# Hi casts of the second FFN's weight sums on GpSimd, three output pairs in the first pass, and a line of their own for gate tiles

## The chip, the cores and the metric

The kernel runs on one core of one Trainium2 chip. The metric is the device time of one execution in microseconds (us), lower is better. Several runs are timed; their median is the time of the kernel. A profiled execution gives the trace.

The engines have short names in the trace: PE is TensorE's matmul and PEld its weight load, DVE is VectorE, ACT is ScalarE, POOL is GpSimd, SP is SyncE, which issues the DMAs. Each engine works through its instructions in the order in which the program has them; an instruction that must wait holds all that stand behind it on its engine.

## The reference

Windowed attention (4 batches, 8 heads, 576 positions, head dimension 64, a window of 64), then two feed-forward networks over the 2304 tokens of 512 features, all in float32:

```python
attn = softmax(where(0 <= i - j < 64, q @ k.T / 8, -1e9)) @ v   # per batch and head
x = attn, heads side by side                                    # 2304 x 512
h = x @ w_in                                                    # 512 -> 2048
x = where(h > 0, h, exp(min(h, 0)) - 1) @ w_out                 # ELU, 2048 -> 512
xn = x / sqrt(mean(x * x, -1) + 1e-6) * rms_g
g, val = xn @ w_gate, xn @ w_val                                # 512 -> 1536 each
out = (g * sigmoid(g) * val) @ w_out2                           # 1536 -> 512
```

## The kernel before

**Precision.** Every operand of the large products is split in two: Hi is the value cast to a narrower matmul type (F32R), Lo is the rest, value minus Hi, cast likewise. A product is then three matmul groups, Hi Hi, Hi Lo and Lo Hi. A split is therefore a cast and a subtraction that reads the cast's result.

**First pass.** Five blocks of tokens (384, 384, 512, 512, 512). In each, 16 steps f make the input product (PE L729), the ELU on ScalarE and VectorE (L767, L769, L771), its split (Hi cast L775, Lo L777), and two steps later the output product (PE L806), which adds up in four PSUM banks y. Attention for the tokens of later blocks is scattered between these steps. When a block ends, its four banks are copied (L839), and the RMS norm follows within the next block; the normed tokens go to DRAM. The 32 split weight units of this FFN stay in SBUF in the 32 slots of the pool "wu". In the last block they come free one by one, and the same slots then serve the second FFN.

**Second pass.** The second FFN works on three superblocks of 768 tokens and computes each 2 x 2 block product with seven products of sums and differences instead of eight (a Strassen scheme; ORDER lists the seven). So it needs seven sums of every weight tile, each split in Hi and Lo. These sums are prepared once, during the first pass and the start of the second, and spilled to DRAM: 12 gate and value units (prep_steps) into pspill, and 6 output pairs (prep_out) into ospill. The second pass loads them back (p_load, o_load). For each superblock it runs three pairs of gate and value tiles (pair, PE L1141), then a half of the output products over these three pairs (outs, PE L1237), then the same for the other three. The third to fifth output pair (counted from 0) serve only the second half. Gate results are kept in tiles G, in slots of "wu"; outs makes sums of them (L1184) and splits these (L1199 Hi, L1202 Lo, the latter on VectorE or GpSimd as the order chooses).

**Preparing a unit or a pair.** Two raw tiles are loaded (L663), their low half words are moved by GpSimd (L669), a join on VectorE (L676) makes the float32 tile in one of two buffers "wm", GpSimd makes four sums of quarter tiles (L1016), and put_out does for each of the seven sums: a Hi cast on ScalarE (L972), a Lo subtraction on GpSimd (L974), and a store by SP (L977), out of one of two buffers "stg". Raw tiles lie in one of three buffers "big4", which the norm uses as well, or, for the output pairs prepared in the second pass, in slots of "wu". A load step calls Feeder.load, which loads every raw tile up to its own that hasn't been loaded.

**The order.** The program order of all engines is made by a list scheduler, class Plan, before anything is built. Each step has a cost for each engine that may run it, the tiles it reads and writes, and for a load the time to landing. Plan.run takes the step that can start first; among those within 0.1 us it prefers the one with the longest tail of work behind it, to which plan.sooner(by, ...) adds some us. Buffers of a pool are counted; Plan.queue puts some tiles in a line, in which a tile gets a buffer only when all those named before it have had theirs. The costs are only used to make the order: on the chip the engines run that order with semaphores.

Of the kernel before, what the change touches and what calls it, by code (L numbers as in the profile page):

```python
# [29 lines left out]
class Plan:  # L30
# [15 lines left out]
        fn()  # L46
        self.early = 0.0

    def add(self, costs, fn, reads=(), writes=(), load=0.0, rows=128, name=None):
        x = Step()  # L50
        x.early = self.early
        x.costs = {e: c * self.MARGIN.get(e, 1.0) for e, c in costs.items()}
        x.fn, x.index, x.load, x.rows, x.name = fn, len(self.steps), load, rows, name
        x.deps, x.tiles = {}, []
        for r in reads:
            key, off = r if isinstance(r[0], tuple) else (r, 0.0)
            self.tile_of(x, key)
            if key in self.writer:
                self.dep(x, self.writer[key], off)
            self.readers.setdefault(key, []).append(x.index)  # L60
        for w in writes:
            key, off = w if isinstance(w[0], tuple) else (w, 0.0)
            self.tile_of(x, key)
            for y in [*self.readers.pop(key, ()), *([self.writer[key]] if key in self.writer else ())]:
                if y != x.index:
                    self.dep(x, y, off)
            self.writer[key] = x.index
        self.steps.append(x)
# [10 lines left out]
    def queue(self, t):  # L79

        if t[0] == "wu":
            return ("raw" if t[1][0] == "r" else "wl" if t[1][0] in ("p", "o") else
                    "wu" if isinstance(t[1], tuple) else None)
        if t[0] == "y" and isinstance(t[1][0], int):
            return "y"
        return None if t[0] in "wy" else t[0]
# [66 lines left out]
    def put(self, x, e, t):  # L153
# [14 lines left out]
        self.free[e] = t + c  # L168
        if x.load:
            self.dma = max(t + 1.6, self.dma) + x.load  # L170
            self.end[x.index] = self.dma + 0.3
        else:
            self.end[x.index] = t + c
        for tile in x.tiles:
# [61 lines left out]
def kernel(  # L236
# [17 lines left out]
    nc = tc.nc  # L254
# [89 lines left out]
    plan = Plan()  # L344
# [620 lines left out]
    def put_out(dst, dkey, src, key, sg, cost={"POOL": 0.82}):  # L965


        def tile_():
            return get((*sg, 0), lambda: mp.tile(
                [128, 2, 256], F32R, tag=sg[0], name=sg[0], bufs=2))  # L970

        add({"ACT": 0.41}, lambda e: nc.scalar.copy(out=tile_()[:, 0, :], in_=src()),  # L972
            reads=[key], writes=[(*sg, "h")])
        add(cost, lambda e: on(e).tensor_tensor(  # L974
            out=tile_()[:, 1, :], in0=src(), in1=tile_()[:, 0, :].bitcast(F32),
            op=ALU.subtract), reads=[key, (*sg, "h")], writes=[(*sg, "l")])
        add({"SP": 0.55}, lambda e: nc.sync.dma_start(out=dst, in_=tile_().bitcast(F32)),  # L977
            reads=[(*sg, "h"), (*sg, "l")], load=0.7, writes=[dkey])

    def prep_steps(t):  # L980

# [51 lines left out]

    def prep_out(i):
        ns = [2 * preps.index(("o", i)) + a for a in range(2)]
        raw = [("wu", ("ro", n), 0) if i >= 4 else ("big4", ("r", n), 0) for n in ns]
        m = [(f"wm{n % 2}", ("p", n)) for n in ns]
        one, sk = ("wm2", "top", 0), ("sw", ("o", i), 0)

# [214 lines left out]
    for f in range(F1):  # L1254
        if f + 1 < F1:
# [3 lines left out]
    OF = [f for i in range(NP2) for f in (i, i + NP2)]  # L1259
    nblk = len(BLOCKS1)  # L1260
    preps = [("p", t) for t in range(4 * (nblk - 2))] + [("o", i) for i in range(NP2)]
    PREP = [{}, *[{f: 4 * b + n for n, f in enumerate((3, 6, 9, 12))}
              for b in range(nblk - 2)],
            {5: 12, 8: 13, 11: 14, 13: 15}]
    w2src = []
    for kind, i in preps:
        for a in range(2):
# [76 lines left out]
    for sb in range(NSB):  # L1344
# [3 lines left out]
        def put(at, fn):  # L1348
            todo.setdefault(at, []).append(fn)
# [15 lines left out]
        if sb == 0:  # L1365
            norm = norm_steps(nblk - 1, BLOCKS1[-1], tok0 - BLOCKS1[-1], True)
            next(norm)
            put(2, lambda: plan.sooner(100.0, lambda: next(norm, None)))
            for i in range(4, NP2):
                put(2 * (i - 4), lambda i=i: plan.sooner(0.0, lambda: prep_out(i)))  # L1370
        if sb + 1 < NSB:
            put(38, lambda: x_load(sb + 1))
            for j, fn in enumerate(x_items(sb + 1)):
# [102 lines left out]
```

## Time and profile before

| | |
|---|---|
| median of 3 runs | 917.25 us (915.98 to 918.17) |
| profiled execution | 915.95 us, span from the first to the last instruction 914.2 us |
| mean granted TensorE clock | 0.994 of full speed |
| TensorE busy with matmuls | 891.2 us, 97% of the span |
| VectorE, ScalarE, GpSimd busy | 632.4, 489.3 and 345.9 us |
| first pass, second pass | the first output product of the last block ends near 502 us; the second FFN's products run from there on |

A busy time is the time in which an engine has an instruction running; TensorE's matmuls are pipelined, so its busy time does not say that each runs at its best. A granted clock of 1.00 is 2.4 GHz, 0.5 is 1.2 GHz; a stretch between has some of both. In a timeline, the bracket behind a row gives how long the engine was idle before it and whose work ended that idle time.

### The profile page before, as it was taken

How to read it: one execution, taken by the hardware profiler on the slowest of the kernel's cores; microseconds unless marked ns; L12 is line 12 of the kernel's file. 1: busy time of each engine (PE TensorE's matmuls, PEld its weight loads, DVE VectorE, ACT ScalarE, POOL GpSimd, SP SyncE). 2: the span in 40 equal slices, each digit the busy share in tenths (PEclk: the TensorE clock that was granted, in tenths of full speed). 3: DMA queues.
4: the chain of work that ended last, by engine and by line, in shares of the span. 5: the costliest groups of instructions: out<-in, count | busy, mean ns of one | idle time of the engine just before them, and what ended most of it. 6: DMA issues, size and time to landing. Idle time of an engine off the chain costs nothing.

```text
span 914.2 us, 16974 instructions
## 1 busy us (share of the span) xinstructions
PE 891.2 (97%) x6063; PEld 824.5 (90%) x6063; DVE 632.4 (69%) x1294; ACT 489.3 (54%) x1191; POOL 345.9 (38%) x379
## 2 busy tenths in 40 slices
PE   8899999999999999999998998999999999999998
PEld 7888999998888888888886998899999999999998
DVE  6899977555656567557755588879758379667476
ACT  6788676765557565546434645445333344333432
POOL 3777632334433442443146557623112113112121
PEclk9999999999999999999998999999999999999999
DMA  9995227735376344837664985994997675988742
GB/s 232 324 330 141 58 81 226 197 108 149 128 240 170 115 141 128 245 129 228 228 235 159 325 303 208 334 410 172 378 359 270 227 244 166 392 300 290 242 149 70
DMA packets 156164, 201.87 MB, mean 221 GB/s; under 512 B 82608, under 2 KB 108720, under 8 KB 156080
## 3 DMA queue, kind: packets, MB, share of 16 engines
q1 hardware_dynamic: 156080, 200.79, 67.2%
q8 instruction: 48, 0.79, 0.4%
q14 instruction: 36, 0.29, 0.1%
HBM read 158.29 MB, written 42.47 MB: 220 GB/s over the span
## 4 chain that ended last, share of the span: by engine, by line
PE 85%; DVE 7%; DMA 3%; ACT 3%; issue 1%; POOL 1%; SPq 0%; DVEq 0%; POOLq 0%; ACTq 0%
PE w L729 19%; PE y L806 19%; PE y L1141 16%; PE w L1141 12%; PE y L1237 8%; PE w L1237 4%; PE w L555 2%; PE w L476 2%; PE w L540 1%; PE w L421 1%; DVE wm L676 1%; DMA ospill<-stg 1%; DVE g L1202 1%; DVE g L777 1%; DMA kq<-in_k_dram 1%
## 5 line engine op out<-in xcount | busy, mean ns | idle before, releaser
L806 PE MATMUL y<-g,wu 128*128 128x512 f32 (+1 forms) x960 | 216.9, 376 | 7.0 <-ACT g L775 4.4
L729 PE MATMUL w<-x,wu 128*128 128x512 f32 (+1 forms) x960 | 212.4, 372 | 2.1 <-POOL wu L692 1.0
L806 PEld LDWEIGHTS y<-g,wu 128*128 128x128 f32 x960 | 174.5, 190 | 32.4 <-ACT g L775 5.3
L729 PEld LDWEIGHTS w<-x,wu 128*128 128x128 f32 x960 | 173.6, 188 | 26.9 <-issue 1.7
L1141 PE MATMUL y<-xw,pu 128*128 128x384 f32 x648 | 121.1, 335 | 0.0
L1141 PEld LDWEIGHTS y<-xw,pu 128*128 128x128 f32 x648 | 112.9, 188 | 0.0
L1114 DVE TENSOR_TENSOR c<-c,w 128x384 f32<-128x384 f32 x72 | 39.7, 553 | 86.0 <-PE w L1141 81.7
L974 POOL TENSOR_TENSOR stg<-wm,stg 128x256 fp32r<-128x256 f32 x70 | 58.7, 840 | 97.1 <-ACT stg L972 95.9
L771 DVE SCALAR_TENSOR_TENSOR e<-e,w 128x512 f32<-128x512 f32 (+1 forms) x80 | 50.2, 631 | 51.9 <-ACT e L769 51.3
L1202 POOL TENSOR_TENSOR g<-slot,g 128x384 fp32r<-128x384 f32 x21 | 27.0, 1286 | 151.9 <-ACT g L1199 108.2
L777 DVE TENSOR_TENSOR g<-e,g 128x512 fp32r<-128x512 f32 (+1 forms) x80 | 67.6, 849 | 24.3 <-ACT g L775 23.7
L1141 PE MATMUL w<-xw,pu 128*128 128x384 f32 x432 | 81.5, 336 | 0.0
L1141 PEld LDWEIGHTS w<-xw,pu 128*128 128x128 f32 x432 | 75.9, 189 | 0.2
L767 ACT ACTIVATE e<-w 128x512 f32<-128x512 f32 (+1 forms) x80 | 44.2, 552 | 57.8 <-PE w L729 57.0
L974 POOL TENSOR_TENSOR stg<-sw,stg 128x256 fp32r<-128x256 f32 x50 | 40.8, 817 | 77.9 <-ACT stg L972 77.9
L1118 DVE TENSOR_TENSOR slot<-slot,c 128x384 f32<-128x384 f32 x108 | 64.0, 604 | 0.9
L1109 ACT COPY c<-y 128x384 f32<-128x384 f32 x72 | 34.4, 480 | 52.1 <-PE y L1141 49.1
L1237 PE MATMUL y<-wu,g 128*128 128x256 f32 x432 | 57.8, 287 | 3.6 <-DVE g L1202 3.4
L1237 PEld LDWEIGHTS y<-wu,g 128*128 128x128 f32 x432 | 54.8, 194 | 4.8 <-DVE g L1202 4.2
L775 ACT CAST g<-e 128x512 fp32r<-128x512 f32 (+1 forms) x76 | 43.7, 575 | 24.4 <-DVE e L771 24.0
L1129 ACT ACTIVATE slot<-c 128x384 f32<-128x384 f32 x54 | 28.4, 526 | 52.0 <-DVE c L1114 50.6
L692 POOL TENSOR_TENSOR wu<-wm,wu 128x512 fp32r<-128x512 f32 x32 | 49.8, 1579 | 14.5 <-ACT wu L687 11.5
(169 smaller groups left out, 1552.5 us busy)
## 6 DMA issues: line engine op xcount, KB each, us to landing
pu<-pspill SPq DMA_DIRECT2D x126, 512.0 KB, 5.9
wu<-ospill SPq DMA_DIRECT2D x60, 512.0 KB, 6.7
pspill<-stg SPq DMA_DIRECT2D x84, 256.0 KB, 2.1
tmp<-in_moe_w_out_dram SPq DMA_DIRECT2D x23, 511.8 KB, 6.8
ospill<-stg SPq DMA_DIRECT2D x36, 256.0 KB, 3.2
tmp<-in_moe_w_in_dram SPq DMA_DIRECT2D x16, 511.0 KB, 7.4
vw<-in_v_dram SPq DMA_DIRECT2D x27, 256.0 KB, 4.2
big<-in_moe_w_gate_dram SPq DMA_DIRECT2D x12, 511.0 KB, 3.8
```

The lines of the kernel that those rows point to most:

```text
L692: nc.gpsimd.tensor_tensor(out=u[:, 1, :], in0=m, in1=u[:, 0, :].bitcast(F32), op=ALU.subtract)
L729: nc.tensor.matmul(pt[:, :n], lhsT=wt[:, a, kk * 128:(kk + 1) * 128], rhs=xs[kk][:, c, :n], start=(i == 0), stop=(i == len(seq) - 1))
L767: add({"ACT": of_n(0.49, n)}, lambda e: nc.scalar.activation(out=et(), in_=ph(), func=AF.Relu, scale=-1.0), reads=ws, writes=[e_])
L771: add({"DVE": of_n(0.56, n)}, lambda e: nc.vector.scalar_tensor_tensor(out=et(), in0=et(), scalar=-1.0, in1=ph(), op0=ALU.add, op1=ALU.max ...
L775: lambda e: copy_on(e)(out=gt()[:, 0, :n], in_=et()),
L777: add({"DVE": of_n(0.68 if b else 0.93, n)}, lambda e: nc.vector.tensor_tensor(out=gt()[:, 1, :n], in0=et(), in1=gt()[:, 0, :n].bitcast(F3 ...
L806: nc.tensor.matmul(py[m][:, :n], lhsT=wt[:, a, m * 128:(m + 1) * 128], rhs=g[:, c, :n], start=(first and i == 0), stop=(last and i == 2))
L974: add(cost, lambda e: on(e).tensor_tensor(out=tile_()[:, 1, :], in0=src(), in1=tile_()[:, 0, :].bitcast(F32), op=ALU.subtract), reads=[key ...
L1114: add({"DVE": 0.55}, lambda e: nc.vector.tensor_tensor(out=c_of(ck), in0=c_of(ck), in1=at(bk), op=ALU.add), reads=[bk], writes=[ck])
L1118: add({"DVE": 0.55}, lambda e: nc.vector.tensor_tensor(out=et(), in0=et(), in1=src_of(sk), op=ALU.mult), reads=[sk], writes=[ek])
L1141: nc.tensor.matmul(at(bk), lhsT=p_of(sb, i, j)[:, qi, a, kk * 128:(kk + 1) * 128], rhs=X_of(sb, j, kk)[:, x, :], start=(first and n == 0), ...
L1237: nc.tensor.matmul(at(bk)[:, (m % 2) * 256:(m % 2) * 256 + 256], lhsT=S_of(jp, i)[:, a, m * 128:(m + 1) * 128], rhs=w[:, x * 256:(x + 1) * ...
```

## The change

The Hi cast of each weight sum is issued on GpSimd (gpsimd.tensor_copy) instead of ScalarE; the scheduler counts 0.82 us for it instead of 0.41. The scheduler counts 0.5 us more until the store of a sum has landed. The last block has three output pairs in its list, not four; the fourth is prepared in the second pass with its raw tiles in slots of "wu", as the last two were, and these three are put at places 0, 12 and 24 of the first superblock, each with 40 us of preference, where the last two had places 0 and 2 and none. Tiles G have a line of their own in Plan.queue; before, they stood in the line of all other slots. PREP for the middle blocks is the same list written out.

```diff
--- before.py
+++ after.py
@@ -46,11 +46,12 @@
         fn()
         self.early = 0.0
 
-    def add(self, costs, fn, reads=(), writes=(), load=0.0, rows=128, name=None):
+    def add(self, costs, fn, reads=(), writes=(), load=0.0, rows=128, name=None, slow=0.0):
         x = Step()
         x.early = self.early
         x.costs = {e: c * self.MARGIN.get(e, 1.0) for e, c in costs.items()}
         x.fn, x.index, x.load, x.rows, x.name = fn, len(self.steps), load, rows, name
+        x.slow = slow
         x.deps, x.tiles = {}, []
         for r in reads:
             key, off = r if isinstance(r[0], tuple) else (r, 0.0)
@@ -80,7 +81,7 @@
 
         if t[0] == "wu":
             return ("raw" if t[1][0] == "r" else "wl" if t[1][0] in ("p", "o") else
-                    "wu" if isinstance(t[1], tuple) else None)
+                    "G" if t[1][0] == "G" else "wu" if isinstance(t[1], tuple) else None)
         if t[0] == "y" and isinstance(t[1][0], int):
             return "y"
         return None if t[0] in "wy" else t[0]
@@ -168,7 +169,7 @@
         self.free[e] = t + c
         if x.load:
             self.dma = max(t + 1.6, self.dma) + x.load
-            self.end[x.index] = self.dma + 0.3
+            self.end[x.index] = self.dma + 0.3 + x.slow
         else:
             self.end[x.index] = t + c
         for tile in x.tiles:
@@ -969,13 +970,13 @@
             return get((*sg, 0), lambda: mp.tile(
                 [128, 2, 256], F32R, tag=sg[0], name=sg[0], bufs=2))
 
-        add({"ACT": 0.41}, lambda e: nc.scalar.copy(out=tile_()[:, 0, :], in_=src()),
+        add({"POOL": 0.82}, lambda e: nc.gpsimd.tensor_copy(out=tile_()[:, 0, :], in_=src()),
             reads=[key], writes=[(*sg, "h")])
         add(cost, lambda e: on(e).tensor_tensor(
             out=tile_()[:, 1, :], in0=src(), in1=tile_()[:, 0, :].bitcast(F32),
             op=ALU.subtract), reads=[key, (*sg, "h")], writes=[(*sg, "l")])
         add({"SP": 0.55}, lambda e: nc.sync.dma_start(out=dst, in_=tile_().bitcast(F32)),
-            reads=[(*sg, "h"), (*sg, "l")], load=0.7, writes=[dkey])
+            reads=[(*sg, "h"), (*sg, "l")], load=0.7, slow=0.5, writes=[dkey])
 
     def prep_steps(t):
 
@@ -1033,7 +1034,7 @@
 
     def prep_out(i):
         ns = [2 * preps.index(("o", i)) + a for a in range(2)]
-        raw = [("wu", ("ro", n), 0) if i >= 4 else ("big4", ("r", n), 0) for n in ns]
+        raw = [("wu", ("ro", n), 0) if i >= 3 else ("big4", ("r", n), 0) for n in ns]
         m = [(f"wm{n % 2}", ("p", n)) for n in ns]
         one, sk = ("wm2", "top", 0), ("sw", ("o", i), 0)
 
@@ -1259,9 +1260,7 @@
     OF = [f for i in range(NP2) for f in (i, i + NP2)]
     nblk = len(BLOCKS1)
     preps = [("p", t) for t in range(4 * (nblk - 2))] + [("o", i) for i in range(NP2)]
-    PREP = [{}, *[{f: 4 * b + n for n, f in enumerate((3, 6, 9, 12))}
-              for b in range(nblk - 2)],
-            {5: 12, 8: 13, 11: 14, 13: 15}]
+    PREP = [{}, {3: 0, 6: 1, 9: 2, 12: 3}, {3: 4, 6: 5, 9: 6, 12: 7}, {3: 8, 6: 9, 9: 10, 12: 11}, {5: 12, 8: 13, 11: 14}]
     w2src = []
     for kind, i in preps:
         for a in range(2):
@@ -1366,8 +1365,8 @@
             norm = norm_steps(nblk - 1, BLOCKS1[-1], tok0 - BLOCKS1[-1], True)
             next(norm)
             put(2, lambda: plan.sooner(100.0, lambda: next(norm, None)))
-            for i in range(4, NP2):
-                put(2 * (i - 4), lambda i=i: plan.sooner(0.0, lambda: prep_out(i)))
+            for i, at in zip(range(3, NP2), (0, 12, 24)):
+                put(at, lambda i=i: plan.sooner(40.0, lambda: prep_out(i)))
         if sb + 1 < NSB:
             put(38, lambda: x_load(sb + 1))
             for j, fn in enumerate(x_items(sb + 1)):
```

## Rows read from the trace of the kernel before

**Rows 1.** The page's part 1: busy us (share) and instructions by engine.

```profile
PE 891.2 (97%) x6063; PEld 824.5 (90%) x6063; DVE 632.4 (69%) x1294; ACT 489.3 (54%) x1191; POOL 345.9 (38%) x379
```

**Rows 2.** Busy us (x instructions) by stretch and engine, granted clock, DMA share, GB/s.

```profile
200.00:300.00 100.00, 100.00 (x685) 82.49 (x685) 58.44 (x156) 61.85 (x165) 40.10 (x51) 1.00 0.56 164
450.00:500.00 50.00, 45.59 (x192) 36.98 (x191) 27.10 (x37) 21.35 (x43) 25.94 (x31) 0.95 0.62 218
500.00:545.00 45.00, 45.00 (x251) 44.21 (x250) 29.00 (x48) 25.62 (x55) 23.95 (x27) 0.98 0.85 296
545.00:580.00 35.00, 30.27 (x218) 29.26 (x218) 30.66 (x43) 14.76 (x37) 21.07 (x22) 0.95 0.73 268
```

**Rows 3.** Timeline, first FFN's end: start us, us, engine, line, work, [idle before <-releaser].

```profile
467.55 0.89 POOL L974 TENSOR_TENSOR stg<-sw,stg 128x256 fp32r<-128x256 f32 x1 [1.03 <-ACT stg L972]
...
469.58 3.05 SPq L663 DMA_DIRECT2D tmp<-in_moe_w_out_dram  x2
...
475.44 0.86 SPq L977 DMA_DIRECT2D ospill<-stg  x2
...
480.75 0.41 ACT L972 CAST stg<-wm 128x256 fp32r<-128x256 f32 x1 [8.53 <-DMA ospill<-stg]
...
482.01 0.69 DVE L676 SCALAR_TENSOR_TENSOR wm<-big,top 128x512 int32<-128x512 int32 x1 [9.07 <-POOL stg L974]
...
489.41 3.02 PE L806 MATMUL y<-g,wu 128*128 128x512 f32 x12 [0.83 <-ACT g L775]
...
496.01 5.49 PE L806 MATMUL y<-g,wu 128*128 128x512 f32 x12 [3.58 <-ACT g L775]
```

**Rows 4.** Chain that ended last, same end and later: start us, us, what.

```profile
475.44 5.23 DMA ospill<-stg
...
482.00 4.28 DMA ospill<-stg
...
620.25 2.16 PE y L1237 x18
```

**Rows 5.** Timeline, first output products of the second FFN (columns as in rows 3).

```profile
551.24 0.62 PE L1237 MATMUL y<-wu,g 128*128 128x256 f32 x3 [1.12 <-DVE g L1202]
...
552.52 2.56 PE L1237 MATMUL y<-wu,g 128*128 128x256 f32 x13 [0.66 <-DVE g L1202]
...
554.88 3.12 PE L1237 MATMUL y<-wu 128*128 128x256 f32 x18
...
561.21 2.18 PE L1237 MATMUL y<-wu 128*128 128x256 f32 x16 [0.80 <-DVE wu L1202]
...
578.35 1.34 PE L1237 MATMUL w<-wu,g 128*128 128x256 f32 x9 [2.13 <-DVE slot L1399]
```

**Rows 6.** Groups of instructions by line: busy us, mean ns | idle before them <-releasers.

```profile
L974 POOL TENSOR_TENSOR stg<-wm,stg 128x256 fp32r<-128x256 f32 x70 | 58.7, 840 | 97.1 <-ACT stg L972 95.9 <-DMA ospill<-stg 0.9
...
L972 ACT CAST stg<-wm 128x256 fp32r<-128x256 f32 x70 | 28.1, 403 | 22.7 <-DMA ospill<-stg 15.7 <-DMA pspill<-stg 4.5 <-DVE wm L676 2.2
...
L669 POOL CAST top<-big 128x512 f16<-128x512 bf16 x29 | 24.8, 855 | 60.0 <-DMA big<-in_moe_w_val_dram 29.0 <-DMA big<-in_moe_w_out_dram 18.1 <-DVE wm L676 9.0
...
L1300 POOL MEMSET top<- 128x512 f32 x1 | 0.5, 522 | 0.0
```

**Rows 7.** Waits by pairs over the span: us in total, times, longest us.

```profile
POOL stg L974 <- ACT stg L972: 173.8, 72, 12.1
...
ACT stg L972 <- DMA ospill<-stg: 19.3, 11, 8.5
```

**Rows 8.** Lines L777, L771: duration ns min/median/max, first and last start us, shapes.

```profile
L777 DVE TENSOR_TENSOR g<-e,g x80: 544/693/1650, 32.2 to 496.0; 128x512 fp32r<-128x512 f32 x48, 128x384 fp32r<-128x384 f32 x32
...
L771 DVE SCALAR_TENSOR_TENSOR e<-e,w x80: 540/680/690, 30.3 to 494.6; 128x512 f32<-128x512 f32 x48, 128x384 f32<-128x384 f32 x32
```

**Rows 9.** Lines L676, L1202 (columns as in rows 8), some of their forms.

```profile
L676 DVE SCALAR_TENSOR_TENSOR wm<-tmp,top x7: 679/683/1223, 497.6 to 581.5; 128x512 int32<-128x512 int32 x7
...
L1202 DVE TENSOR_TENSOR wu<-slot,wu x9: 543/546/1080, 552.4 to 565.5; 128x384 fp32r<-128x384 f32 x9
```

## The prediction

> **What bounds the kernel now.** I read the page's first part, then the busy times by stretch, the timelines of the two stretches that show idle TensorE, the chain of waits through them, and the waits summed by pairs.
>
> TensorE is busy for 891.2 of 914.2 us [rows 1]. The stretches tell the rest [rows 2]: from 200 to 300 us TensorE is idle for nothing at a granted clock of 1.00; from 450 to 500 it is busy for 45.6 of 50 us, and from 545 to 580 for 30.3 of 35, both at a mean granted clock of 0.95, that is, part of the time at 1.2 instead of 2.4 GHz. So what a change outside the matmuls can give back lies in these two stretches, and what it can spoil is the first pass, which loses nothing today.
>
> Loss A is the end of the first FFN [rows 3]. TensorE waits 0.83 us and 3.58 us for an activation's Hi cast, and then the product at 496.01 takes 5.49 us where the one at 489.41 took 3.02 us: 2.47 us to the lower clock, which fell behind the wait. A = 0.83 + 3.58 + 2.47 = 6.9 us. Its cause stands in the same timeline. ScalarE's cast L972 for the spilled weight sums starts at 480.75 after 8.53 us of waiting for a store, and the ELU's first step L767 stands behind it in ScalarE's queue. VectorE has its own wait to the same moment: the join L676 at 482.01 waits 9.07 us for GpSimd's subtraction L974, because the join overwrites what L974 reads, and the ELU's step L771 stands behind the join. The store itself was late: GpSimd had finished its source at 467.55 + 0.89 = 468.44, but SP issued it at 475.44, behind raw loads (L663) which waited for weight slots, and the chain of waits runs through it and the next store for 5.23 and 4.28 us [rows 4].
>
> Loss B is the first half of the second FFN's output products [rows 5]: waits of 1.12, 0.66 and 0.80 us for VectorE's Lo parts, and the lower clock, 18 matmuls in 3.12 us against 2.16 at full clock [rows 4], and 13 in 2.56 us against 13/18 of 2.16 = 1.56. B = 2.58 + 0.96 + 1.00 = 4.5 us. Loss C is the 2.13 us wait at 578.35 for VectorE's sum L1399. VectorE is busy for 30.7 of the 35 us there [rows 2].
>
> **The change, part by part.** *The casts.* 126 casts leave ScalarE (seven for each of 12 gate and value units and 6 output pairs), each about 403 ns [rows 6]: 51 us less of an engine that is 54% busy, worth nothing by itself. What counts is the wait before them, 19.3 us for output stores [rows 7], which holds the ELU; on GpSimd it holds only the preparation, since in the blocks after the first no ELU step runs there. The trace has no 128x256 cast on GpSimd. From below it is half of the 128x512 memset's 522 ns, 0.26 us; from above the two-input subtraction of the same size, 0.84 us; the nearest row is GpSimd's 128x512 cast of 855 ns, half of which is 0.43 us [rows 6]. I take 0.43: 126 x 0.43 = 54 us (33 to 106) more on an engine that is busy for 345.9 of 914.2 us [rows 1]. One pair has two 0.855 casts, four sums and seven subtractions at about 0.84 us, 10.9 us; with seven casts it has 13.9. Four pairs per first-pass block are 56 us of the 100 in [rows 2], three in the last block 42 us of some 55. So it fits. In exchange GpSimd's 173.8 us of waits for ScalarE's cast [rows 7] shrink: cast and subtraction now follow each other on one queue, with the store's wait ahead of both. What is queued behind that wait on GpSimd is the next sums and, in the second pass, Lo parts (L1202).
>
> The cost on VectorE: its activation Lo L777, which reads two SBUF tiles, takes 544 to 1650 ns, median 693, while L771, which reads one of its two tiles from PSUM, stays between 540 and 690, its two widths [rows 8]. So GpSimd's work stretches VectorE's two-tile work. By the Trainium skill (SBUF — State Buffer, Who interferes with whom) VectorE with two SBUF inputs and a GpSimd instruction that reads SBUF exclude each other for a whole instruction, and ScalarE has ports of its own; these rows agree, and by that rule moving the cast off ScalarE is a loss for VectorE wherever it is full. By another page of the Trainium skill (GPSIMD Engine Reference, Engine selection) one-input work there runs near line rate; no row shows a cast of this size, and an estimate from it, 256 elements at 1.2 GHz, would be 0.21 us and the sum over 126 casts 27 us instead of 54. In the first pass VectorE is 58% busy and the output product comes two steps behind the ELU, so I cost the stretching at nothing there; were that cover gone, a collision would cost up to 0.4 us on TensorE (the cast's length). In the full stretch from 545 to 580 about seven casts of one pair fall, 7 x 0.43 = 3.0 us, of which I let a third reach TensorE: +1.0 us (between 0 and 3.0).
>
> *Three pairs instead of four in the last block.* Less moves than the words say. All 12 output raws are loaded in order, and a load step that comes up early loads all before it as well, into its own kind of buffer: seven of the twelve are joined out of weight slots ("tmp"), where four were meant to be, and these joins run from 497.6 to 581.5 us [rows 9]. So before the change only two pairs and the start of a third are prepared in the first pass. Now six raws are meant for slots and counted there. The load, join, cast, sum and store instructions stay as many, SP's too. Zero, with a gain contained in A: fewer loads that the order did not count stand in SP's queue ahead of the stores.
>
> *The store's extra 0.5 us and the new cast cost in the order of work.* Both enter the order written out, not the chip. A staged sum is counted 0.41 + 0.5 = 0.9 us later, seven of them 6.4 us, about one ELU step of the last block (two products, 2 x 3.02 us [rows 3]). The join that waited 9.07 us is therefore put behind one ELU step more, and about 2.7 us of its wait would be left, less than the two steps by which the output product trails. With the cast gone from ScalarE's queue and the join later in VectorE's, both holds of A go: -6.9 us (between -6.9 and 0).
>
> *Own order of places for activations.* Gate tiles no longer stand in one line with raw loads. In the pairs' stretch from 500 to 545 us TensorE is busy for 45.0 of 45 us [rows 2], so I take 0. The sixth pair's raws still stand in line behind second-output tiles, whose Lo parts first run at 552.4 [rows 9]. Loaded from there (some 5 us, like the stores of rows 4), joined and prepared for 13.9 us with as much again of store waits, it is out by 590; its consumer starts at 620.25 [rows 4]. That slack of 30 us covers it; beyond it each us would be one of TensorE.
>
> **The sum.** A -6.9, B +1.0, C 0, the first pass 0: -5.9 us. The profiled execution took 915.95 us (span 914.2 and 1.75 around it), so 910.05; it lies 1.3 us below the median 917.25 of the runs, and against that median I predict 911.3 us.
>
> **The rivals.** *R1, the hold only changes queue.* The store is late because of SP, so GpSimd waits for it instead of ScalarE, the join still waits for GpSimd to 482, and the ELU's L771 is as late as before. For it: VectorE's wait of 9.07 us ends at the same moment as ScalarE's 8.53 [rows 3], so freeing one alone gives nothing. Against: the order of the joins changes too. Time: 917.25 + 1.0 - about 1 = 917.3.
>
> *R2, the second pass becomes the bound (slower).* With cast and subtraction both on GpSimd, the order gives its Lo parts to VectorE, and the two pairs prepared around 545 to 580 us collide with it. VectorE has 35 - 30.7 = 4.3 us to spare there. Four Lo parts moved, at 0.55 us unhindered [rows 9], are 2.2 us; 14 casts x 0.43 = 6.0 us of collisions, 8.2 in all, 3.9 over the room, and a further clock fall like the one in B, 1.0 to 2.0 us: +5.4. With A unrecovered as in R1, 922.6; it decides from the point where VectorE's busy share there passes 35 us. For it: B and C are waits for VectorE already. Against: the casts may be short and ScalarE, with 14.8 of 35 us, can take copies.
>
> *R3, everything late goes.* A, B and C together, 6.9 + 4.5 + 2.1 = 13.5: 903.8. For it: the last-block norm gets its buffers earlier when a pair less holds them. Against: B's VectorE is full for other reasons.
>
> **How the numbers follow.** The forecast has 0.48 (907 to 915), R1 0.18, R2 0.21, R3 0.13. About 0.2% (1.8 us) is what a measurement can tell from no change. Forecast and R3 count as faster, 0.61; R1 as the same, 0.18; R2 as slower, 0.21. The range takes R3's 903.8 with 2 us for an unknown first half, and R2's 922.6: 902 to 923.
>
> **What would show it.** Right: no L972 on ScalarE; a cast on GpSimd of about 0.43 us; no wait of several us before L767 between 450 and 500 us, joins there waiting under 3 us, and a granted clock of 1.00. Wrong: TensorE's waits for L775 at the block's end as long as before (R1), more than 2.6 us of waits for L1202 in the second pass's first output half (R2), any idle TensorE between 200 and 450 us, or a cast near 0.84 us, which would make a first-pass block's GpSimd 67 us and bring the joins near the block's end.

## The result and the profile after

| | before | after |
|---|---|---|
| median | 916.62 us (914.88 to 918.17, 4 runs) | 904.98 us (903.76 to 906.14, 4 runs) |
| profiled execution, its span | 915.95 and 914.2 us | 906.14 and 904.4 us |
| TensorE without work in the span | 914.2 - 891.2 = 23.0 us | 904.4 - 887.7 = 16.7 us |

The changed kernel is faster, by a ratio of 0.9876 [0.9855, 0.9898]. That is 11.6 us where 5.9 us were forecast: inside the range, in the forecast direction, but twice its size, and next to R3's 903.8. The profiled execution after is the longest of its four, so its trace shows 9.8 us of the 11.6.

Part 1 of the page of the kernel after (busy us, share, instructions by engine) answers to [rows 1]:

```profile
PE 887.7 (98%) x6063; PEld 821.6 (91%) x6063; DVE 638.2 (71%) x1302; ACT 450.0 (50%) x1068; POOL 398.3 (44%) x494
```

ScalarE has lost 39 us and GpSimd has gained 52: that part of the change did what it says. TensorE's own busy time fell by 3.5 us for as many matmuls, with a mean granted clock of 0.996 instead of 0.994. The same four stretches as in [rows 2] (busy us and instructions of PE, PEld, DVE, ACT, POOL, then granted clock, DMA share, GB/s) say where it came from:

```profile
200.00:300.00 100.00, 100.00 (x684) 82.27 (x683) 60.36 (x154) 53.43 (x138) 58.30 (x86) 1.00 0.60 171
450.00:500.00 50.00, 50.00 (x229) 42.29 (x228) 24.54 (x35) 20.49 (x37) 35.34 (x52) 1.00 0.62 211
500.00:545.00 45.00, 43.54 (x255) 42.34 (x253) 40.98 (x64) 18.74 (x37) 26.99 (x30) 1.00 0.84 312
545.00:580.00 35.00, 32.93 (x223) 31.91 (x224) 25.84 (x38) 13.06 (x30) 26.24 (x35) 0.95 0.85 309
```

From 200 to 450 us TensorE is busy without a gap in both. The stretch of loss A is full, at a granted clock of 1.00. And VectorE has changed its stretch: 29.0 before, now 41.0 us between 500 and 545 us, and 30.7 before, now 25.8 between 545 and 580. Nothing in the forecast was about that.

The moments at which TensorE reaches the same place of the program, read from the starts of its matmuls in the two profiled executions, divide the gain:

| TensorE (us) | before | after | gained so far | in this part |
|---|---|---|---|---|
| starts the last block | 405.91 | 406.84 | -0.93 | -0.93 |
| ends the first FFN's last output product | 501.50 | 494.95 | 6.55 | 7.48 |
| starts the second FFN's output products | 546.22 | 541.01 | 5.21 | -1.34 |
| starts the second half of these products | 620.09 | 612.86 | 7.23 | 2.02 |
| starts the second superblock | 644.64 | 635.53 | 9.11 | 1.88 |
| starts the third superblock | 778.05 | 768.24 | 9.82 | 0.71 |

The first FFN's last output product is the one near 502 us; the table of the time before calls it the first. Loss A went, as forecast. The second superblock's start gained 3.9 us on top (2.02 + 1.88), in the place where the forecast had a loss of 1.0.

The timeline of the kernel after, at the end of the first FFN (start, us, engine, line, work, idle before it and the releaser; SPq is SP's queue of DMAs, and lines stand one higher than before):

```profile
465.06 0.33 SPq L664 DMA_DIRECT2D tmp<-in_moe_w_out_dram  x1
465.45 0.40 POOL L973 CAST stg<-wm 128x256 fp32r<-128x256 f32 x1 [2.40 <-DMA ospill<-stg]
466.70 0.32 SPq L978 DMA_DIRECT2D ospill<-stg  x1
...
467.78 3.05 SPq L664 DMA_DIRECT2D tmp<-in_moe_w_out_dram  x2
...
472.53 0.33 SPq L978 DMA_DIRECT2D ospill<-stg  x1
...
483.29 0.68 DVE L677 SCALAR_TENSOR_TENSOR wm<-big,top 128x512 int32<-128x512 int32 x1
...
486.63 8.32 PE L807 MATMUL y<-g,wu 128*128 128x512 f32 x36
...
494.35 1.08 ACT L840 COPY big<-y 128x512 f32<-128x512 f32 x2 [3.30 <-DMA ospill<-stg]
494.54 1.29 DVE L840 COPY big<-y 128x512 f32<-128x512 f32 x2 [2.71 <-PE y L807]
```

The cast on GpSimd waits 2.40 us for a store where ScalarE's waited 8.53, joins do not wait, and 36 matmuls of the output product follow each other without a gap [rows 3]. Two things here return in the experiments: SP never has more than two raw loads for slots ("tmp") between two stores, and all four copies of the last block's banks (L840) have run by 496 us.

What is left of waiting, in the timeline of the kernel after from 508 to 580 us:

```profile
514.87 2.38 PE L1142 MATMUL y<-x,pu 128*128 128x384 f32 x12 [1.35 <-DVE c L1115]
...
546.08 1.29 PE L1238 MATMUL y<-wu,g 128*128 128x256 f32 x6 [1.18 <-DVE g L1203]
547.75 2.36 PE L1238 MATMUL y<-wu,g 128*128 128x256 f32 x10 [0.38 <-DVE g L1203]
```

The first is new, 1.35 us for VectorE in the stretch that it now fills. Losses B and C had 2.58 and 2.13 us of waits; two of 1.18 and 0.38 remain, one of 0.39 at 566.4, and 3.4 us at half clock (granted 0.50 from 548 to 551) behind the first two.

The cast itself, by its line (duration ns min/median/max; six more go to tiles "e"):

```profile
L973 POOL CAST stg<-wm x70: 387/402/945, 115.0 to 597.3; 128x256 fp32r<-128x256 f32 x70
L973 POOL CAST stg<-sw x50: 390/402/939, 124.4 to 587.1; 128x256 fp32r<-128x256 f32 x50
```

### The profile page after: what moved, and what is told of

The parts are those of the page before. It is cut to its first block, busy times and chain, and to the rows that moved or that the text cites. A ratio compares the mean times of both kernels' runs of the same rounds, so it can differ in the third digit from the quotient of the medians.

```text
span 904.4 us, 16833 instructions
## 1 busy us (share of the span) xinstructions
PE 887.7 (98%) x6063; PEld 821.6 (91%) x6063; DVE 638.2 (71%) x1302; ACT 450.0 (50%) x1068; POOL 398.3 (44%) x494
## 4 chain that ended last, share of the span: by engine, by line
PE 87%; DVE 5%; SPq 3%; DMA 2%; issue 1%; ACT 1%; POOL 0%; POOLq 0%; DVEq 0%
PE y L807 20%; PE w L730 20%; PE y L1142 16%; PE w L1142 12%; PE y L1238 9%; PE w L1238 5%; SPq L330 2%; PE w L556 2%; PE w L477 2%; PE w L541 1%; SPq L664 1%; PE w L422 1%; DMA kq<-in_q_dram 1%; DVE wm L677 1%; DMA vw<-in_v_dram 1%
## 5 line engine op out<-in xcount | busy, mean ns | idle before, releaser
L973 POOL CAST stg<-wm 128x256 fp32r<-128x256 f32 x70 | 37.9, 541 | 57.3 <-DMA pspill<-stg 39.4
L670 POOL CAST top<-big 128x512 f16<-128x512 bf16 x30 | 24.8, 827 | 78.1 <-DMA big<-in_moe_w_val_dram 32.1
```

Source lines behind the costliest of these rows:

```text
L973: add({"POOL": 0.82}, lambda e: nc.gpsimd.tensor_copy(out=tile_()[:, 0, :], in_=src()), reads=[key], writes=[(*sg, "h")])
```

## The experiments

My theory after seeing these traces had three parts: the new order of work, not the cast, brings the gain; loss A hangs on how many raw loads stand in a row in SP's queue; and the gain behind 541 us comes from buffers that the norm gets earlier. The rival was the prediction's: the cast leaving ScalarE ends loss A. Each batch ran beside the kernel before on its own chip, and ratios are to those runs. The diffs are cut to the lines that carry the edit. Each kernel has one trace, and readings from it are of that execution.

**The cast alone, in the old order.** Every instruction but the cast keeps its place; the scheduler still counts 0.41 us on ScalarE.

```diff
 # kernel before
-        add({"ACT": 0.41}, lambda e: nc.scalar.copy(out=tile_()[:, 0, :], in_=src()),
+        add({"ACT": 0.41}, lambda e: nc.gpsimd.tensor_copy(out=tile_()[:, 0, :], in_=src()),
```

> The kernel before with one edit: the Hi cast of the weight sums runs on GpSimd, while the scheduler still counts it as 0.41 us on ScalarE, so that the order on TensorE, VectorE and SP is that of before, line for line. Theory 1 (ScalarE's wait is what holds the ELU at the first FFN's end): the 6.9 us of loss A go, about 910 us. Theory 2 (R1: VectorE's join waits to the same moment, and the store is as late as before): within 2 us of before, 915 to 918 us, and the join near 482 us still waits some 9 us. Theory 3 (only the remade order counts): the same as theory 2.

Measured: 919.77 us, 1.0052 [1.0035, 1.0068], slower. Its timeline at the end of the first FFN:

```profile
468.85 5.67 SPq L663 DMA_DIRECT2D tmp<-in_moe_w_out_dram  x4
...
482.50 0.40 POOL L972 CAST stg<-wm 128x256 fp32r<-128x256 f32 x1 [9.76 <-DMA ospill<-stg]
...
483.75 0.69 DVE L676 SCALAR_TENSOR_TENSOR wm<-big,top 128x512 int32<-128x512 int32 x1 [8.91 <-POOL stg L974]
...
498.13 2.08 PE L806 MATMUL y<-g,wu 128*128 128x512 f32 x4 [4.93 <-ACT g L775]
```

For loss A this is R1, step by step. Four raw loads stand in one row in SP's queue, each waiting for a slot that TensorE has yet to leave; the store behind them is late; the cast waits for it on GpSimd as it did on ScalarE, the join waits for the subtraction, and TensorE waits 4.93 us. ScalarE's freedom is worth nothing. But R1 forecast no change in time, and this is 4.5 us slower: in its trace TensorE needs 2.7 us more from the first output product of the second FFN to the second half of these products (76.56 instead of 73.87 us), where R2 and the term B +1.0 had put collisions on VectorE.

**The cast alone, with its cost in the order.**

```diff
 # kernel before
-        add({"ACT": 0.41}, lambda e: nc.scalar.copy(out=tile_()[:, 0, :], in_=src()),
+        add({"POOL": 0.82}, lambda e: nc.gpsimd.tensor_copy(out=tile_()[:, 0, :], in_=src()),
```

> The kernel before with the cast on GpSimd and its cost of 0.82 us known to the scheduler; four pairs, the old line for gate tiles, no extra 0.5 us. Theory 1 (cast and its order carry the gain): at least two thirds of the measured 11.6 us, 905 to 909 us. Theory 2 (the pairs and the line carry it): 914 to 918 us.

Measured: 917.96 us, 1.0033 [1.0020, 1.0047], slower. The other order has three raw loads in a row instead of four, ends most of A (5.5 us in the trace) and loses it again; its timeline around 625 us:

```profile
624.37 0.47 ACT L1129 ACTIVATE slot<-y 128x384 f32<-128x384 f32 x1
...
628.00 3.43 PE L1237 MATMUL y<-wu,g 128*128 128x256 f32 x12 [4.73 <-ACT g L1199]
```

The last sigmoid of the first superblock's sixth pair runs at 624.37, and TensorE has nothing for 4.73 us. The next runs explain it.

**The new order, the cast back on ScalarE.**

```diff
 # kernel after
-        add({"POOL": 0.82}, lambda e: nc.gpsimd.tensor_copy(out=tile_()[:, 0, :], in_=src()),
+        add({"POOL": 0.82}, lambda e: nc.scalar.copy(out=tile_()[:, 0, :], in_=src()),
```

> The changed kernel with one edit: the cast is executed by ScalarE again, at the place that the order has for it on GpSimd. Theory 1 (what the cast's engine does on the chip carries the gain): A comes back, 911 to 918 us. Theory 2 (the order alone carries it): 904 to 907 us.

Measured: 904.03 us, 0.9874 [0.9856, 0.9892], as fast as the change itself as far as the medians tell.

**Three pairs, their places and the line for G, without cast and store term.**

```diff
 # kernel before
+                    "G" if t[1][0] == "G" else "wu" if isinstance(t[1], tuple) else None)
-        raw = [("wu", ("ro", n), 0) if i >= 4 else ("big4", ("r", n), 0) for n in ns]
+        raw = [("wu", ("ro", n), 0) if i >= 3 else ("big4", ("r", n), 0) for n in ns]
-            {5: 12, 8: 13, 11: 14, 13: 15}]
+    PREP = [{}, {3: 0, 6: 1, 9: 2, 12: 3}, {3: 4, 6: 5, 9: 6, 12: 7}, {3: 8, 6: 9, 9: 10, 12: 11}, {5: 12, 8: 13, 11: 14}]
-            for i in range(4, NP2):
-                put(2 * (i - 4), lambda i=i: plan.sooner(0.0, lambda: prep_out(i)))
+            for i, at in zip(range(3, NP2), (0, 12, 24)):
+                put(at, lambda i=i: plan.sooner(40.0, lambda: prep_out(i)))
```

> The kernel before with three output pairs in the last block, the places 0, 12 and 24 with 40 us of preference, and the gate tiles' own line; the cast stays on ScalarE and the store's extra 0.5 us is left out. Theory 1 (the cast carries the gain): 913 to 917 us, with a wait of several us of ScalarE for a store near the block's end. Theory 2 (the pairs and the line carry it): 905 to 909 us.

Measured: 904.84 us, 0.9884 [0.9867, 0.9900]. This is the whole gain, with every cast on ScalarE. Its timeline at the end of the first FFN:

```profile
476.59 0.41 ACT L972 CAST stg<-wm 128x256 fp32r<-128x256 f32 x1 [4.56 <-DMA ospill<-stg]
...
477.85 0.69 DVE L676 SCALAR_TENSOR_TENSOR wm<-big,top 128x512 int32<-128x512 int32 x1 [5.10 <-POOL stg L974]
...
491.37 3.02 PE L806 MATMUL y<-g,wu 128*128 128x512 f32 x12 [0.26 <-ACT g L775]
```

With two raw loads in a row instead of four the same kind of wait for a store is still there, 4.56 us, and the join's 5.10, but the output product, two steps behind, feels 0.26 us of it.

**The line alone, the pairs alone.** The first has only the "G" line of the diff above, the second all of it but that line.

```diff
 # kernel before, line alone
+                    "G" if t[1][0] == "G" else "wu" if isinstance(t[1], tuple) else None)
 # kernel before, pairs without the line: prep_out, PREP and the places as in the diff above
+            for i, at in zip(range(3, NP2), (0, 12, 24)):
+                put(at, lambda i=i: plan.sooner(40.0, lambda: prep_out(i)))
```

> The kernel before with only the gate tiles' own line. Theory 1 (the line lets gate tiles and second-output tiles be placed earlier, which shortens the later waits for Lo parts, while A is untouched): 909 to 913 us, with A's waits near 490 us as before. Theory 2 (the gain is that of the pairs): 914 to 917 us.

> The kernel before with three output pairs in the last block and the places 0, 12 and 24 with 40 us of preference, but the old line for gate tiles; cast on ScalarE. Theory 1 (pairs end A, the line ends the later waits): 907 to 911 us, with no wait over 1 us near 490 us and waits for Lo parts left in the second pass. Theory 2 (the pairs carry all of it): 903 to 906 us.

Measured: the line alone 913.89 us, 0.9974 [0.9959, 0.9989]; the pairs alone 916.67 us, 1.0004 [0.9990, 1.0017]. One is worth 2.6 us, the other nothing, both together 10.4 (the run before): what they give isn't a sum. The line alone leaves A's wait of 3.6 us, B and C [rows 3, 5]; what goes are waits of 0.22 and 1.15 us at the second superblock and 0.45 us at the third. The pairs alone end A, and lose it all again at the turn to the second superblock; their timeline there:

```profile
613.03 0.51 ACT L924 CAST xw<-xa 128x384 fp32r<-128x384 f32 x1
...
624.17 0.51 ACT L924 CAST xw<-slot 128x384 fp32r<-128x384 f32 x1
624.58 0.52 ACT L1129 ACTIVATE slot<-c 128x384 f32<-128x384 f32 x1
625.01 0.47 ACT L1129 ACTIVATE slot<-y 128x384 f32<-128x384 f32 x1
...
628.86 3.43 PE L1237 MATMUL y<-wu,g 128*128 128x256 f32 x12 [4.13 <-ACT g L1199]
```

The sixth pair's last sigmoids stand behind casts of the next superblock's X on ScalarE. With the line (three pairs, places and line, the run before) the last of them runs at 609.69, and TensorE passes the same place without a wait:

```profile
609.69 0.49 ACT L1129 ACTIVATE slot<-y 128x384 f32<-128x384 f32 x1 [0.53 <-PE y L1141]
...
626.72 2.32 PE L1237 MATMUL y<-wu,big 128*128 128x256 f32 x18
```

So with the old line the last sigmoid runs 15 us later. A reading of the order that no run follows slot by slot: in the old line the G tiles stand behind the raw tiles of the late pairs, of which there is now one pair more.

**Loads in order.** Here each raw load step of the weights that are prepared waits in the scheduler for the one before it, so that none loads several, and the pairs, the places and the line stay as before.

```diff
 # kernel before
-        add({"SP": 0.55}, go, writes=[tile], load=1.45,
+        add({"SP": 0.55}, go, writes=[tile] + ([(("seq", "fwp", 0), 100.0)] if f is fwp else []), load=1.45,
```

> The kernel before, where a load step of a raw tile may only be placed after the load step before it, so that no step loads others' tiles into weight slots that the scheduler did not count (eight raws in big4 buffers and four in slots, as meant). Theory 1 (A comes from the four raw loads in a row on SP ahead of the store): A's 6.9 us go, 907 to 911 us. Theory 2 (A comes from four pairs being too many for the block, wherever their raws lie): 913 to 918 us, the join near 480 us waiting several us still.

Measured: 912.08 us, 0.9954 [0.9936, 0.9972]. A is gone; the first of these joins waits

```profile
476.66 0.69 DVE L676 SCALAR_TENSOR_TENSOR wm<-big,top 128x512 int32<-128x512 int32 x1 [0.94 <-POOL stg L974]
```

and where B and C stood there are waits of 1.11, 2.02, 0.66 and 1.93 us. 4.4 us in the median is what is left when A is ended in this way; it is not A's price, since the new order gives 3.8 us back between the first output product and the second half (77.64 instead of 73.87 us). (In its profiled execution, the longest of 12, the last block starts 4.2 us late, and the first FFN then ends 7.5 us earlier against that.)

**Places alone.** Four pairs as before, only the late two put at places 12 and 24 with 40 us of preference.

```diff
 # kernel before
-                put(2 * (i - 4), lambda i=i: plan.sooner(0.0, lambda: prep_out(i)))
+                put(12 * (i - 3), lambda i=i: plan.sooner(40.0, lambda: prep_out(i)))
```

> The kernel before, four pairs in the last block, where the last two pairs are put at places 12 and 24 with 40 us of preference instead of 0 and 2 without. Their raw loads then come after the last block, and those of the fourth pair lie in big4 as meant. Theory 1 (what counts is which raw loads stand in the last block's SP queue): A's 6.9 us go, 907 to 911 us. Theory 2 (what counts is the fourth pair's preparation itself): 913 to 918 us.

Measured: 914.73 us, 0.9990 [0.9980, 1.0000], the interval touching no change. The last output product ends 7 us earlier, so A went here too; then there are waits where B stood, and 1.86 and 1.19 us at 622 to 626, the place at which the pairs without the line lose theirs.

**Four pairs with the line, loads in order; four pairs with the line and the new places.** These two ask whether the fourth pair matters once A is gone, and whether A comes back.

```diff
 # kernel before, the first
+                    "G" if t[1][0] == "G" else "wu" if isinstance(t[1], tuple) else None)
+        add({"SP": 0.55}, go, writes=[tile] + ([(("seq", "fwp", 0), 100.0)] if f is fwp else []), load=1.45,
 # kernel before, the second
+                    "G" if t[1][0] == "G" else "wu" if isinstance(t[1], tuple) else None)
+                put(12 * (i - 3), lambda i=i: plan.sooner(40.0, lambda: prep_out(i)))
```

> The kernel before with four pairs, the gate tiles' own line, and raw loads in their order. Theory 1 (A is the raw loads ahead of the store in SP's queue, the later losses are the gate tiles' place; the number of pairs in the first pass does not matter): 903 to 907 us, as with the pairs and the line. Theory 2 (the third pair's move is needed as well, because it makes the last block's norm and the sums early): 909 to 912 us, with waits for Lo parts near 550 and 570 us left.

> The kernel before with four pairs in the last block, the last two at places 12 and 24 with 40 us of preference, and the gate tiles' own line. The order has the four raw loads in a row into weight slots again, as before. Theory 1 (A is these four loads ahead of the store): A is back, 908 to 913 us, with a join that waits over 5 us near 480. Theory 2 (A is the number of pairs that the last block has to get through): A is back as well, but with the join's wait ended by GpSimd's sums rather than by a store. Theory 3 (the places and the line carry the gain): 903 to 907 us.

Measured: 911.01 us, 0.9941 [0.9923, 0.9960], and 913.22 us, 0.9961 [0.9947, 0.9975]. In the second the four raw loads are in one row again, and A with them, whatever the places are; its timeline:

```profile
465.88 7.35 SPq L663 DMA_DIRECT2D tmp<-in_moe_w_out_dram  x4
...
482.38 0.41 ACT L972 CAST stg<-wm 128x256 fp32r<-128x256 f32 x1 [9.55 <-DMA ospill<-stg]
...
483.64 0.69 DVE L676 SCALAR_TENSOR_TENSOR wm<-big,top 128x512 int32<-128x512 int32 x1 [10.09 <-POOL stg L974]
...
496.90 3.38 PE L806 MATMUL y<-g,wu 128*128 128x512 f32 x10 [3.58 <-ACT g L775]
```

The first has no A and the line, and still lacks 6 us against three pairs with the line, the places and the same load order (905.01, below). Two of its last block's bank copies wait for a join that reads out of "big4" until 512.59, and the clock falls to 0.90 from 545 to 580 us. That VectorE is full there, 31.45 of 35 us, can't be the cause by itself: with three pairs, the line and the old places (below) it is busy for 32.78 us and TensorE for all 35. The three rows, the last two with columns as in [rows 2]:

```profile
512.59 1.07 ACT L839 COPY big<-y 128x512 f32<-128x512 f32 x2 [4.16 <-DVE wm L676]
```

```profile
545.00:580.00 35.00, 30.59 (x209) 29.73 (x210) 31.45 (x40) 14.18 (x34) 22.62 (x22) 0.90 0.75 266
```

```profile
545.00:580.00 35.00, 35.00 (x243) 34.90 (x242) 32.78 (x54) 19.02 (x46) 18.98 (x19) 0.95 0.76 272
```

What goes with the late loss is where nine steps of the last block's norm (L855, L857, L860, three times) stand in VectorE's order. In the kernel before they stand among the output products, right behind the third cast into a tile "e" and right ahead of the sum that TensorE waits for in loss C:

```profile
567.72 0.41 ACT L972 CAST e<-sw 128x256 fp32r<-128x256 f32 x1 [1.62 <-POOL sw L1016]
568.54 1.10 DVE L855 TENSOR_TENSOR e<-big 128x512 f32<-128x512 f32 x1
...
577.27 0.69 DVE L860 SCALAR_TENSOR_TENSOR big<-e,big 128x512 f32<-128x512 f32 x1
577.88 0.75 DVE L1399 TENSOR_TENSOR slot<-slot,w 128x256 f32<-128x256 f32 x2
```

In the kernel with four pairs, places and line they run ahead of the output products, which start at 547.47:

```profile
530.29 0.68 DVE L855 TENSOR_TENSOR e<-big 128x512 f32<-128x512 f32 x1
...
538.04 0.69 DVE L860 SCALAR_TENSOR_TENSOR big<-e,big 128x512 f32<-128x512 f32 x1
...
570.28 0.40 ACT L972 CAST e<-sw 128x256 fp32r<-128x256 f32 x1
```

The program gives a reason. The norm's temporary is a tile "e"; the fifth and sixth pair (counted from one) stage three of their seven sums in tiles "e" as well, and "e" has a line in Plan.queue. With the old list the fifth pair stands at place 0, the norm's second part at place 2, so the norm's temporary comes behind the fifth pair's three tiles. With three pairs the fourth pair, which uses "stg" alone, takes place 0; with the new places the fifth goes to 12. Either way the norm comes first. The traces, in us, the first two columns at the start of an instruction, the last two from matmul start to matmul start (second half means that of the output products; the 24.85 has six matmuls of the second superblock in it):

| kernel | third cast into "e" | norm's first L855 | first output product to second half | second half to second superblock |
|---|---|---|---|---|
| before | 567.72 | 568.54 | 73.87 | 24.55 |
| loads in order | 562.95 | 563.36 | 77.64 | 24.55 |
| line alone | 567.14 | 567.96 | 75.45 | 22.67 |
| line, loads in order | 559.05 | 559.46 | 76.03 | 24.85 |
| places alone, four pairs | 563.42 | 523.30 | 73.03 | 29.49 |
| places and line, four pairs | 570.28 | 530.29 | 71.93 | 22.67 |
| three pairs, places | 565.34 | 505.59 | 72.84 | 33.09 |
| three pairs, places, line | 561.85 | 504.11 | 70.97 | 22.67 |
| the change | 564.72 | 506.05 | 71.85 | 22.67 |

In the traces of all fourteen kernels the first half is shorter where the norm stands ahead of the products (69.69 to 73.03 us, with three pairs or four) than where it stands among them (73.87 to 77.64), and the line takes the loss out of the second half. Buffers do delay the norm with four pairs: their last bank copy starts at 505 to 518 us, with three all copies have run by 497. But with the new places that alone does not push it behind the products' start. So four pairs with places and line have the whole late gain and lack only what comes before it, against the three pairs with the line, the places and loads in order: 6.5 us of A and 1.2 us ahead of the products.

**Three pairs and the line, old places; and all of it with the loads in order.**

```diff
 # kernel before, the first: line, prep_out and PREP as in three pairs, and
-            for i in range(4, NP2):
-                put(2 * (i - 4), lambda i=i: plan.sooner(0.0, lambda: prep_out(i)))
+            for i in range(3, NP2):
+                put(2 * (i - 3), lambda i=i: plan.sooner(0.0, lambda: prep_out(i)))
 # the second: three pairs, places and line, and
+        add({"SP": 0.55}, go, writes=[tile] + ([(("seq", "fwp", 0), 100.0)] if f is fwp else []), load=1.45,
```

> The kernel before with three pairs in the last block and the gate tiles' own line; the last three pairs stand at places 0, 2 and 4 without preference. Theory 1 (three pairs and the line are enough): 903 to 907 us. Theory 2 (the places and the preference are needed): 909 to 914 us, the sixth pair's raw loads standing in the last block's SP queue again, A at least half back.

> Three pairs, the line and the new places, cast on ScalarE, and raw loads in their order, the candidate for a version that beats both. Theory 1 (what is left of A, ScalarE's and the join's waits of about 5 us near 480, is already hidden): 903.5 to 905.5 us, the same as without the load order. Theory 2 (the last raw that lies in the wrong kind of buffer still costs): 900 to 903 us.

Measured: 903.96 us, 0.9865 [0.9844, 0.9886], and 905.01 us, 0.9875 [0.9856, 0.9894]. With three pairs the places and the preference add nothing: at place 2 the fifth pair is already named behind the norm, whose L855 starts at 505.05. And once only two loads stand in a row, ordering them adds nothing either. The first of the two has the lowest ratio of all; against the change's 0.9876 [0.9855, 0.9898] that isn't a difference, but it gets there with two edits instead of five.

## Why the prediction was half right

**A, right in place and size, wrong in cause.** Forecast 6.9, measured 7.5 us between the last block's start and the end of its output products. But the step "With the cast gone from ScalarE's queue and the join later in VectorE's, both holds of A go" doesn't hold as I put it. The cast gone from ScalarE leaves 4.93 us of A (cast alone), and A ends with the cast on ScalarE too (three pairs, loads in order, places alone). What goes with A in every run is SP's queue between 455 and 500 us: four raw loads for slots in a row, over 5.7 to 7.4 us, in the four kernels that have A (before, cast alone in the old order, line alone, four pairs with line and places), at most three in all others. My clause that fewer such loads would stand ahead of the stores was right; I made it a side gain of the pairs, and let the cast and the order's costs decide. Of the two the cost has a part: with the cast and its cost alone the row is three loads long and 5.5 of the 7.5 us go. The store's 0.5 us was not tried by itself; three pairs and the line reach the same time without it.

**"*Three pairs instead of four* [...] Zero, with a gain contained in A": the step that failed.** I counted the instructions that move and found none that cost, but not who takes the place that comes free, in front of whom. The fourth pair takes place 0 and the fifth goes behind the norm, so nine VectorE steps of the norm start at 506.05 instead of 568.54, in a stretch where VectorE had 16 of 45 us to spare. The part up to the second half of the output products becomes 2.02 us shorter, and the price of it is the new wait of 1.35 us at 513.5, where TensorE waits for VectorE behind these steps. Four pairs get the same first half from the places (71.93 us), so the number of pairs isn't the cause of this. That the norm's place is, is read from the program and agrees with every trace; no run changes that place alone.

**R3, near the time by luck.** Its 903.8 us stood on A, B and C all going, because the norm gets its buffers earlier. The norm did come earlier, by its place in the line for "e" and with bank copies done by 496 us. But B's waits lie at 551 to 561 us, ahead of the norm's steps, and two of 1.18 and 0.38 us are still in its place: my objection that VectorE is full there for other reasons held for B. It failed for C, which stood right behind the norm. The rest of the gain behind 541 us came from the line, which R3 did not have.

**B +1.0 and C 0: wrong sign.** B, C and the waits of 0.22 and 1.15 us at 627 to 629 us, for which the sum had no term, make a part that became 3.9 us shorter [rows 5]. The collisions that I priced at 1.0 us (0 to 3.0) are hidden in it. Where only the cast's engine differs they show in the traces up to the second half: 2.7 us between the kernel before and the cast alone in the old order, 2.2 us between the new order with the cast on ScalarE (69.69) and the change (71.85). The medians show the first, not the second.

**"*Own order of places for activations* [...] I take 0": also failed.** I looked at the stretch from 500 to 545 us, where TensorE was busy throughout, and at the sixth output pair's slack, but not at what the G tiles do later in the line. Alone it gives 2.6 us, in the change's trace 1.88 in the second half and 0.71 in the second superblock. With three pairs it is what keeps their gain: without it 916.67, with it 904.84 us.

**The cast.** 0.43 us was forecast, the median is 0.40, and from 200 to 450 us TensorE is busy without a gap with it. Its worth was misjudged: with the new order the cast's engine makes no difference that the medians show (904.98 against 904.03, overlapping ratios), and alone it costs 0.3 to 0.5%. R2's fear, a VectorE over its room from 545 us on, did not come true in the change, since the norm's steps have left that stretch; in the cast alone, where they stay, a part of it did.

By the Trainium skill (SBUF — State Buffer, Who interferes with whom) a VectorE instruction with two SBUF inputs and a GpSimd instruction that reads SBUF shut each other out. The cast's spread from 387 to 945 ns agrees; one of the long ones started beside such a VectorE instruction:

```profile
473.18 0.69 DVE L778 TENSOR_TENSOR g<-e,g 128x512 fp32r<-128x512 f32 x1 [0.69 <-ACT g L776]
473.19 0.94 POOL L973 CAST stg<-sw 128x256 fp32r<-128x256 f32 x1 [0.69 <-DMA ospill<-stg]
```

The estimate of 0.21 us from the Trainium skill (GPSIMD Engine Reference, Engine selection), near line rate, does not agree: 0.40 us is measured, and the measurement decides.

**The sum, corrected.** By terms in the trace: 7.5 for A, -1.3 for the new wait at 513.5, 2.0 in the first half of the output products, 1.9 in the second and 0.7 in the second superblock, -0.9 in the first pass: 9.8. In the median: loads in order, which end A, are worth 4.4 us, the line alone 2.6, and four pairs with both reach 5.6. Three pairs and the places on top of these, which bring the norm forward, give 6.0 more (911.01 against 905.01 us in the same batch); the traces of these two differ by 4.7 us, 4.2 of them in the first half of the products (76.03 and 71.87).

What stays open: why the scheduler, with these pairs and the old line, puts the last G tiles so late was read from the order and from one run with and one without the line; the slots were not followed one by one. The interplay of places with A (places alone end it, places with the line have it back) is a matter of which load step comes up first in the list, and no run isolates it.

## What to carry to other kernels

When work is moved to a later stage, look at every line for buffers that it stood in, not at its instructions alone: ask who moves up, who is now named ahead of whom, and what that one then does earlier. A wait that two engines end at the same moment is not cured on either of them; follow it back to the queue that was late, here loads that wait for buffers ahead of a store that waits for nothing. And try the parts of such a change singly and in pairs: here none alone gives over 2.6 us, the cast alone costs 2.7 to 4.5, and three pairs with the line give it all.

## What the hardware showed

GpSimd's cast of 128x256 from float32 to F32R takes 0.40 us in the median, stretched up to 0.95 us; its 128x512 cast of other types takes 855 ns in the mean [rows 6]; ScalarE does the same cast in 0.40 us, so in the median GpSimd is no slower at this; in the mean, 0.54 and 0.56 us by the tile it reads, it is. A wait of 5.10 us in VectorE's queue cost TensorE 0.26 us, those of 8.83 to 10.09 us cost 3.6 to 4.9: the two steps by which the output product trails hide the one and not the other.
